# A recurrent attention with a token-mixing layer on one Trainium2 core: values of the last batch loaded like all others, ten output buffers, and a new order of 650 steps

## The chip, the core and the metric

The kernel runs on one core of one Trainium2 chip. A core has five engines with an instruction queue each: TensorE (PE in the profile; its weight loads are PEld) multiplies matrices and writes to the accumulator memory PSUM; VectorE (DVE), ScalarE (ACT) and GpSimd (POOL) compute on tiles in on-chip memory; SyncE (SP) here only issues transfers. Sixteen DMA engines carry the transfers between the chip's main memory and the on-chip memory. Every queue is worked in order: an instruction that waits holds all that stand behind it on its engine. The metric is the device time of one execution in microseconds (us), and the median of several runs counts.

## The reference

Four batches, eight heads, 768 tokens, 48 values to a head. The first layer is a recurrence with a decaying state, the second mixes tokens. Cut to what is computed:

```python
B, H, S, D = 4, 8, 768, 48
for t in range(S):
    cur = einsum('bhd,bhe->bhde', u * k[:, :, t], v[:, :, t])
    y[:, :, t] = einsum('bhd,bhde->bhe', r[:, :, t], state + cur)
    state = w[:, :, t, :, None] * state + einsum('bhd,bhe->bhde', k[:, :, t], v[:, :, t])
x = y.transpose(0, 2, 1, 3).reshape(B, S, H * D)
W_tok = einsum('bsd,btd->bst', x @ w_q, x @ w_k) / sqrt(64)
out = maximum(einsum('bst,btd->bsd', W_tok, x), 0) @ w_out
```

Inputs and output are float32; r, k, v and w have 4.7 MB each, and so has the output.

## The kernel before

**Units.** The work is cut into twelve units n = 0 to 11 of 256 tokens, three to a batch (n = 3b + i). A unit takes its tokens as two chunks c of 128. Its steps have names that stand here with their numbers: `kT_6` is the step kT of unit 6, `AM_6_1` the step AM of unit 6, chunk 1.

**First layer of a unit.** Four loads bring w, k, r and v (wg, kg, rg, vg, 384 KB each). ScalarE takes the logarithm (ln), TensorE sums it along the tokens (cw), ScalarE makes the two exponentials ep and en. Casts make k16, r16 and v16 in bf16; TensorE turns k and r (kT, rT). VectorE or ScalarE copies the turned k out of PSUM (ks), VectorE multiplies (qT, RT), and KT is ks (or the turned k in PSUM) times en, on GpSimd or VectorE. v must be permuted among partitions: TensorE does that (vp), and ScalarE copies the result out of PSUM (VB). dps and dd give the factors of the bonus, and Vd is VB times dd on GpSimd. Then A is the product of KT and RT for each chunk, AM masks it (VectorE), kb and kd turn KT back, sn and SB carry the state from chunk to chunk, yi and ya sum the output in PSUM, and X is that sum plus Vd. X is either an addition on VectorE, or TensorE adds Vd into PSUM (step yv) and ScalarE copies.

**Second layer.** xt and XT turn X, qk and QK project it (in the last unit the parts are wk, wq, wkc, wqc). When a batch has its three units, T and TS sum over the batch; then for each unit mx, a relu (rl), fp (the product with w_out), a copy os out of PSUM, and a store st. All the second half of a batch can be put off as long as buffers allow.

**Loads of v.** In units 0 to 8 v comes by `load`: two neighbouring tokens of a head are one run of 384 bytes, and vp permutes. The last batch is in `WHOLE` (line 170): there v comes by four transfers `load_whole` (lines 237 to 241), in runs of 192 bytes, already in permuted order, into one large tile vw of all three units; VB is then a cast from vw on GpSimd or ScalarE (lines 533 to 537) and there is neither v16 nor vp. k and r of all units but the first come by `load_long` in runs of 768 bytes.

**Buffers.** Loads have rings of four buffers (lines 194 to 201), so the load of unit n waits until unit n - 4 has read its buffer. The output tile os has a ring of four as well.

**Weights.** w_q and w_k (wts) and w_out (wo) are loaded on SP's queue, in two transfers each (rows 0 to 99 and 100 to 127) where the way is `T`, in one where it is `S` (lines 343 to 358). Both stand as `T`. wcast and ocast make them bf16.

**The order.** It is written out by hand in three tables (lines 84 to 134): `ORDER` lists the numbers of all steps in the order in which they are put on the engines' queues, `WAYS` the engine or form of each step that has a choice, and `BANKS` the PSUM bank of each tile there. A form `N` does nothing, `e` and `c` are other forms of the same step on TensorE, `d` is KT read from PSUM on VectorE. `WARM` (24) gives steps z, products with a tile of zeros, that keep TensorE busy; in this order 11 of them are done, the rest are `N`. Nine more stand ahead of all steps (line 873).

The queue of SP, decoded:

```
kg_0 wg_0 wg_1 rg_0 kg_1 kg_2 vg_0 rg_1 wg_2 vg_1 wg_3 rg_2 vg_2 kg_3 rg_3 wts vg_3 wg_4 wg_5
kg_4 rg_4 kg_5 rg_5 vg_4 wo wg_6 vg_5 wg_7 rg_6 kg_6 vg_6 kg_7 rg_7 vg_7 wg_8 kg_8 rg_8 wg_9 vg_8
kg_9 rg_9 kg_10 wg_10 rg_10 vw (4 transfers) st_0 wg_11 kg_11 rg_11 st_1 st_2 st_4 st_3 st_5 ...
```

At the end, VectorE does TS_11, four relus (rl_9_0, rl_9_1, rl_11_0, rl_11_1) and os_11_1; ScalarE does rl_10_0, rl_10_1, then os_9_0, os_10_0, os_10_1, os_9_1, os_11_0.

The lines that carry the choice of v, and the copy that follows:

```python
WHOLE = (B - 1,)
...
        if whole:
            VBs = add(("VB", n), "PA", lambda e: copy(
                e, view(VB.tile, 0, [[D, H], [DM, 2], [1, D]]),
                view(batch["vw"].tile, 2 * i * D, [[NCH * D, H], [D, 2], [1, D]])),
                batch["vwL"], VB, [batch["vw"]], cols=2 * DM)
```

Of the kernel before, what the change touches and what calls it, by code (L numbers as in the profile page):

```python
# [10 lines left out]
F32 = mybir.dt.float32  # L11
# [21 lines left out]
class Plan:  # L33
# [9 lines left out]
    def add(self, key, ways, fn, after=(), buf=None, reads=(), cols=0, mode=0, behind=None,  # L43
            half=-1, more=None):
        s = dict(key=key, ways=ways, way=ways[0], fn=fn, after=list(after), buf=buf,
                 reads=list(reads), cols=cols, mode=mode, behind=behind, half=half,
                 more=more or {}, i=len(self.steps), fills=False, out=False)
        if buf is not None:
            if buf.filler is None:
                buf.filler = s  # L50
                s["fills"] = True
                if buf.tile is None:
                    self.banks.append(buf)
                elif behind is None and buf.before is not None:
                    s["behind"] = buf.before.filler
            elif behind is None:
                s["behind"] = buf.filler
        self.steps.append(s)
        return s
# [22 lines left out]


ORDER = [
# [34 lines left out]
]  # L119
WAYS = (  # L120
    "PPDPPDPPDDDDDDPDTTPDDAAPPDPPPADDDEENDEAAPPDdPADEAEENDEAAAPAPPADEDcNDEDAAAAAAAAPADdPAAEAc"
    "cNDEADPPDdPAAeAcENDeDAPPDPPAAeAENDEAAAAAAAAAPPDPPAAEDEENDEAAPPDdPAAeAEENDEAAPPDPPAAEAcND"
    "EDAAADAAAAPPDPPAEAEcNDeAAPPDPPAeAccNDeDAPPDPPPAPPAENDEDADNDEAADDDDAAAAAADDADNNEEEENEEENE"
    "NENENNNNNNEN"
)
BANKS = [
# [7 lines left out]
]  # L134


WARM = 24

# [2 lines left out]
def kernel(  # L141
# [13 lines left out]
    B, H, S, D = r.shape  # L155
# [11 lines left out]
    N = B * NU  # L167

    LONG = tuple(range(1, N))
    WHOLE = (B - 1,)  # L170

    SHIFT = 25
    KAPPA = SHIFT * math.log(2.0)
# [11 lines left out]
    def const(shape, dtype, name):  # L185
# [6 lines left out]
    QW = NU * QS  # L192

    RINGS = dict(
        wg=(4, HW, F32), rg=(4, HW, F32), kg=(4, HW, F32), vg=(4, HW, F32), os=(4, 2 * DM, F32),
        kd=(2, KW, BF16), lw=(2, 1024, BF16), r16=(2, 1024, BF16), k16=(2, 1024, BF16),
        ep=(2, 8 * EW, BF16), en=(2, 1024, BF16), ks=(2, 1024, BF16), qT=(2, 1024, BF16),
        RT=(2, 1024, BF16), KT=(2, 1024, BF16), v16=(2, 2 * DM, BF16), VB=(2, 2 * DM, BF16),
# [139 lines left out]
    wts = {}  # L338

    def dma(key, fn, after=(), buf=None, reads=()):  # L340
        return add(key, "ST" if key[0] in ("wts", "wo") else "S", fn, after, buf, reads)

    def weights():
        def rows(e):
# [561 lines left out]
```

## Time and profile before

| what | value |
|---|---|
| median of 3 runs | 103.6 us |
| lowest, highest run | 101.3, 104.62 us |
| span of the profiled execution, first to last instruction | 101.1 us |
| moved by DMA in it | 24.68 MB, mean 244 GB/s |
| loads landed: median from issue, kg / wg / rg / vg | 5.5 / 6.3 / 6.4 / 6.9 us |
| stores landed: median from issue, 384 KB / 192 KB | 3.2 / 2.8 us |

The profile is of one execution. The page gives its span, and no time beside it; the runs differ from one another by 3.2%. In rows of groups, the first number behind the bar is the busy time of the group in us (overlaps taken out), the second the mean duration of one instruction in ns, and behind the second bar stands the time that the engine idled just before, with what ended it. In rows of time, the columns are start, duration, engine, line, operation, tiles, count, and in brackets the idle time before. In rows of stages, they are the stage, its length, the busy times of PE, PEld, DVE, ACT and POOL, the granted clock of TensorE, the share of the 16 DMA engines' time, and GB/s. The records of two instructions that follow one another on VectorE or ScalarE overlap by some 0.08 us, and a few matmul records are missing.

### The profile page before, as it was taken

What the parts mean: (1) busy time and instruction counts of PE and PEld (TensorE: products, weight loads), DVE (VectorE), ACT (ScalarE), POOL (GpSimd) and SP (SyncE); (2) the same over time, 40 slices, a digit from 0 to 9 for tenths busy, and PEclk for the clock granted to TensorE, in tenths of its full rate; (3) what the DMA queues carried; (4) which work ended last, traced back from release to release, by engine and by line L of the source; (5) the groups of instructions that cost most, each with busy time, mean ns of one, the idle gap of its engine ahead of it and who ended that gap; (6) DMA issues with size and microseconds to landing.
All of it is one profiled execution on the core that took longest, in us unless ns stands there. A gap on an engine that the chain in (4) does not pass through costs nothing.

```text
span 101.1 us, 4474 instructions
## 1 busy us (share of the span) xinstructions
PE 86.8 (86%) x1906; PEld 63.4 (63%) x1909; DVE 80.5 (80%) x134; ACT 80.9 (80%) x134; POOL 68.8 (68%) x82
## 2 busy tenths in 40 slices
PE   5966984989899888999899988999999998999920
PEld 1334553777597556678577875787877667776500
DVE  5423896899999989889999899999997897565520
ACT  5068975999799699599998999989997995735930
POOL 6858964699937764968899749999995897000000
PEclk9999999999999999999999999999999999999999
DMA  1999998999999999999999799999888831007591
GB/s 26 309 324 346 332 317 227 341 261 274 313 306 240 257 205 244 291 329 341 224 323 287 192 343 301 166 155 250 229 233 310 314 141 67 0 0 303 209 366 69
DMA packets 45165, 24.68 MB, mean 244 GB/s; under 512 B 31576, under 2 KB 43992, under 8 KB 45144
## 3 DMA queue, kind: packets, MB, share of 16 engines
q1 hardware_dynamic: 44984, 24.19, 86.9%
q8 instruction: 15, 0.25, 1.0%
q10 hardware_dynamic: 160, 0.20, 0.6%
q14 instruction: 6, 0.05, 0.2%
HBM read 19.66 MB, written 4.72 MB: 241 GB/s over the span
## 4 chain that ended last, share of the span: by engine, by line
PE 34%; ACT 15%; DMA 13%; DVE 12%; SPq 10%; issue 7%; POOL 4%; DVEq 0%; POOLq 0%; ACTq 0%
PE PS L177 34%; DMA vg<-in_v_dram 7%; DMA kg<-in_k_dram 6%; ACT ep L444 6%; SPq L227 5%; ACT en L451 4%; SPq L232 4%; DVE AM L592 3%; DVE X L724 2%; ACT os L275 2%; POOL v L281 2%; DVE ks L281 1%; POOL r L414 1%; DVE RT L513 1%; DVE qT L503 1%
## 5 line engine op out<-in xcount | busy, mean ns | idle before, releaser
L592 DVE TENSOR_TENSOR AM<-PS,US 128x1024 bf16<-128x1024 f32 x24 | 28.7, 1216 | 0.9 <-PE PS L177 0.6
L523 POOL TENSOR_TENSOR KT<-ks,en 128x1024 bf16<-128x1024 bf16 (+1 forms) x10 | 17.4, 1739 | 2.7 <-DVE qT L503 2.0
L572 POOL TENSOR_TENSOR Vd<-VB,dd 128x768 bf16<-128x768 bf16 (+1 forms) x14 | 18.0, 1292 | 1.5 <-ACT dd L275 1.0
L444 ACT ACTIVATE ep<-PS,kp 128x512 bf16<-128x512 f32 (+1 forms) x28 | 16.3, 646 | 0.1
L451 ACT ACTIVATE en<-PS,km 128x1024 bf16<-128x1024 f32 (+1 forms) x14 | 13.9, 1002 | 1.1 <-ACT QK L275 0.8
L724 DVE TENSOR_TENSOR X<-PS,Vd 128x768 bf16<-128x768 f32 (+1 forms) x13 | 11.6, 889 | 2.7 <-POOL Vd L572 1.4
L177 PE MATMUL PS<-wo,MX 128*128 128x384 bf16 x72 | 13.3, 326 | 0.2 <-ACT ep L444 0.2
L177 PEld LDWEIGHTS <-KT 48*128 48x128 bf16 (+1 forms) x312 | 10.3, 94 | 5.1 <-issue 2.6
L177 PE MATMUL PS<-RT,KT 48*128 48x128 bf16 x192 | 9.6, 217 | 1.9 <-POOL KT L523 1.0
L414 POOL CAST k<-kg 128x768 bf16<-128x768 f32 x10 | 8.2, 824 | 3.6 <-DMA kg<-in_k_dram 1.8
L281 DVE COPY ks<-PS 128x1024 bf16<-128x1024 bf16 x11 | 7.6, 689 | 3.7 <-PE PS L177 3.7
L275 ACT COPY os<-PS 128x768 f32<-128x768 f32 (+1 forms) x13 | 8.8, 679 | 1.9 <-PE PS L177 1.6
L414 POOL CAST r<-rg 128x768 bf16<-128x768 f32 x10 | 8.2, 824 | 3.1 <-DMA rg<-in_r_dram 1.9
L513 DVE TENSOR_TENSOR RT<-PS,ep 128x1024 bf16<-128x1024 bf16 (+1 forms) x14 | 8.5, 608 | 2.2 <-ACT ep L444 2.0
L403 ACT ACTIVATE lw<-wg 128x768 bf16<-128x768 f32 x12 | 10.1, 850 | 0.1
L177 PEld LDWEIGHTS <-MX 128*128 128x128 bf16 x72 | 6.4, 97 | 4.3 <-DVE MX L289 0.3
L287 ACT ACTIVATE MX<-PS 128x768 bf16<-128x768 f32 (+1 forms) x11 | 8.2, 758 | 0.9 <-PE PS L177 0.8
L275 ACT CAST VB<-PS 128x768 bf16<-128x768 f32 x9 | 7.3, 806 | 1.8 <-PE PS L177 1.7
L281 POOL CAST v<-vg 128x768 bf16<-128x768 f32 x9 | 7.4, 823 | 1.8 <-DMA vg<-in_v_dram 1.7
L177 PE MATMUL PS<-CM,lw 64*128 64x128 bf16 x192 | 7.9, 217 | 0.7 <-issue 0.4
L656 DVE TENSOR_TENSOR SB<-PS,ep 128x192 bf16<-128x192 f32 x20 | 7.0, 350 | 1.6 <-PE PS L177 1.5
L503 DVE TENSOR_TENSOR qT<-PS,ks 128x1024 bf16<-128x1024 bf16 x12 | 8.2, 681 | 0.0
(82 smaller groups left out, 182.8 us busy)
## 6 DMA issues: line engine op xcount, KB each, us to landing
kg<-in_k_dram SPq DMA_DIRECT2D x12, 384.0 KB, 5.5
wg<-in_w_dram SPq DMA_DIRECT2D x12, 384.0 KB, 6.3
rg<-in_r_dram SPq DMA_DIRECT2D x12, 384.0 KB, 6.4
vg<-in_v_dram SPq DMA_DIRECT2D x9, 384.0 KB, 6.9
out_dram<-os SPq DMA_DIRECT2D x9, 384.0 KB, 3.2
vw<-in_v_dram SPq DMA_DIRECT2D x4, 288.0 KB
out_dram<-os SPq DMA_DIRECT2D x5, 192.0 KB, 2.8
wof<-in_moe_w_out_dram SPq DMA_DIRECT2D x1, 450.0 KB
```

The lines of the kernel that those rows point to most:

```text
L177: return nc.tensor.matmul(o, l, rr, start=start, stop=stop, skip_group_check=True, is_transpose=trans)
L275: nc.scalar.copy(o, i)
L281: x.tensor_copy(o, i)
L403: nc.scalar.activation(view(lw.tile, 0, [[64, H], [512, 2], [1, D]]), view(g["wg"].tile, 0, [[D2, H], [D, 2], [1, D]]), ACT.Ln, bias=0.0, ...
L414: op(view(o.tile, 0, [[64, NP], [256, 4], [1, D]]), view(g[src].tile, 0, [[2 * D2, NP], [D, 4], [1, D]]))
L444: nc.scalar.activation(view(ep.tile, cs[0] * NP * EW + off, [[EW, NP * len(cs)], [step, 2], [1, 32]]), view(at(cw), cs[0] * 512 + j * 64, ...
L451: nc.scalar.activation(en.tile[:, ds(cs[0] * 512, w_)], at(cw)[:, ds(cs[0] * 512, w_)], ACT.Exp, bias=km, scale=-1.0)
L513: nc.vector.tensor_tensor(plain(RT.tile, cs, 32), turned(512, cs, True), plain(ep.tile, cs, EW // 4), ALU.mult)
L523: x.tensor_tensor(KT.tile[:, cols], ks.tile[:, cols], en.tile[:, cols], ALU.mult)
L572: (nc.vector if e == "D" else nc.gpsimd).tensor_tensor(Vd.tile[:, cols], VB.tile[:, cols], view(dd.tile, cs[0] * H, [[1, len(cs) * H], [0, ...
L592: AMs[c] = add(("AM", n, c), "D", lambda e, c=c, A=A: nc.vector.tensor_tensor(view(AM[c].tile, 0, [[C, 8], [1, C]]), view(at(A), 0, [[C, 8 ...
L724: nc.vector.tensor_tensor(o, y_, view(Vd.tile, c0 * DM, dims), ALU.add)
```

## The change

The last batch leaves `WHOLE`, so units 9 to 11 get loads vg, casts v16, products vp and copies VB like the others, and the four vw transfers and the tile vw are gone. The ring os has ten buffers. The weights are loaded by one transfer for each matrix. All three tables are new.

```diff
@@ ORDER, WAYS, BANKS @@
 ORDER = [
-    38, 15, 441, 301, 32, 18, 649, 644, 22, 539, 645, 2, 3, 26, 25, 0, 401, 581, 4, 5, 34, 33, 23,
...
+    37, 38, 39, 40, 86, 85, 87, 128, 88, 127, 129, 14, 21, 0, 2, 5, 12, 32, 22, 10, 4, 3, 7, 24,
...
@@ the kernel @@
     LONG = tuple(range(1, N))
-    WHOLE = (B - 1,)
+    WHOLE = ()
...
     RINGS = dict(
-        wg=(4, HW, F32), rg=(4, HW, F32), kg=(4, HW, F32), vg=(4, HW, F32), os=(4, 2 * DM, F32),
+        wg=(4, HW, F32), rg=(4, HW, F32), kg=(4, HW, F32), vg=(4, HW, F32), os=(10, 2 * DM, F32),
...
     def dma(key, fn, after=(), buf=None, reads=()):
-        return add(key, "ST" if key[0] in ("wts", "wo") else "S", fn, after, buf, reads)
+        return add(key, "S", fn, after, buf, reads)
```

The steps are numbered anew (657 instead of 652, since v now has five steps more). Decoded, SP's queue is:

```
wg_0 kg_0 rg_0 vg_0 kg_1 wg_1 rg_1 kg_2 vg_1 wg_2 rg_2 wg_3 vg_2 kg_3 rg_3 vg_3 wg_4 rg_4 kg_4 wts
wg_5 vg_4 rg_5 kg_5 vg_5 wg_6 kg_6 rg_6 wg_7 kg_7 vg_6 rg_7 vg_7 kg_8 wg_8 rg_8 vg_8 rg_9 wg_9 wg_10
rg_10 kg_9 kg_10 wo vg_9 wg_11 vg_10 vg_11 kg_11 rg_11 st_2 st_0 st_1 st_3 st_5 st_6 st_4 st_7 st_8 ...
```

What goes to which engine (number of steps before -> after, where it differs):

```
TensorE  vp 9 -> 12; yv done 0 -> 3; z done 11 -> 5; kb in form E 6 -> 3, e 7 -> 10;
         xt in form E 10 -> 8, e 3 -> 5; sn in form E 12 -> 11, c 8 -> 9
VectorE  KT 4 -> 7 (KT_0 in two halves among them); X 13 -> 10; dd 3 -> 7; kd 4 -> 6; wkc 0 -> 2;
         rl 4 halves -> 5 halves and 2 whole; os 1 whole and 1 half -> 3 halves; ks 11 -> 10;
         QK 1 -> 2; pads 2 -> 1; IU 1 -> 0
ScalarE  VB 9 -> 12; X 0 -> 3; rl 11 -> 8; kd 9 -> 7; dd 9 -> 5; os 13 -> 12; QK 10 -> 9; ks 1 -> 2;
         wkc 2 -> 0; k16 and r16 1 -> 0; v16 0 -> 1
GpSimd   KT 10 -> 7; VB 3 -> 0; v16 9 -> 11; k16 and r16 11 -> 12; pads 0 -> 1; IU 0 -> 1
```

IU makes the tile IDU, pads clears the tile kd. In the set-up, GpSimd now does 18 instructions ahead of k16_0 (ms_lw0, ms_ep1, ms_kp, ms_U, ms_I, as_C01, as_U1, as_C00, as_U2, ms_km, as_PM, as_ID, IU, pads_1, as_C10, as_C11, as_U0, as_U3; ms is a memset, as a selection by index).

TensorE's queue from the turn of k in unit 10 on, before and after (fp of units 9 and 11 comes in halves):

```
before  kT_10 rT_10 ya_8_1 ya_8_0 fp_3 mx_4 xt_7 xt_8 A_9_0 A_9_1 mx_5 qk_8 kb_9 A_10_0 dps_10 qk_7
        kb_10 sn_9_0 ya_9_0 ya_9_1 A_10_1 yi_9_1 fp_4 sn_9_1 cw_11 kT_11 sn_10_0 rT_11 yi_10_0
        ya_10_0 fp_5 ya_10_1 yi_10_1 xt_9 sn_10_1 T_8 A_11_0 kb_11 xt_10 dps_11 qk_9 mx_6 sn_11_0
        A_11_1 yi_11_0 ya_11_0 mx_7 qk_10 mx_8 yi_11_1 ya_11_1 fp_6 xt_11_0 xt_11_1 fp_7 wk_11_1
        wq_11_1 wk_11_0 wq_11_0 T_11_0 T_11_5 T_11_4 fp_8 mx_9 mx_10 mx_11 fp_9_0 fp_10_0 fp_10_1
        fp_9_1 fp_11_0 fp_11_1
after   kT_10 rT_10 xt_8 fp_1 A_9_1 vp_9 mx_3 fp_2 sn_9_0 A_10_0 dps_10 vp_10 mx_5 sn_9_1 A_9_0 cw_11
        kb_10 fp_0 A_10_1 sn_10_0 qk_8 ya_9_0 ya_9_1 kT_11 yi_9_1 rT_11 fp_5 yi_10_0 yi_10_1 ya_10_0
        ya_10_1 vp_11 T_8 sn_10_1 xt_9 A_11_1 kb_11 fp_3 sn_11_0 dps_11 A_11_0 xt_10 yi_11_0 yi_11_1
        qk_9 ya_11_1 mx_6 qk_10 ya_11_0 mx_4 fp_6 xt_11_0 xt_11_1 mx_7 fp_4 wk_11_0 wk_11_1 mx_8 fp_7
        T_11_0 T_11_4 T_11_5 wq_11_0 wq_11_1 fp_8 mx_11 mx_10 mx_9 fp_11_0 fp_10_0 fp_10_1 fp_11_1
        fp_9_0 fp_9_1
```

On GpSimd, ocast stands behind k16_10 and ahead of v16_9, KT_10 and v16_10. At the end VectorE does TS_11, wqc_11_0, wqc_11_1, rl_11_0, rl_10_0, rl_10_1, os_10_0, rl_9_0, rl_9_1, os_9_0, os_9_1, and ScalarE rl_11_1, os_11_0, os_10_1, os_11_1.

More of the change, by code (lines that the diff above doesn't have):

```diff
@@ L84 @@
 ORDER = [
[34 rows of a table removed]
[36 rows of a table added]
 ]
 WAYS = (
[L121 to L124, printed above, removed]
+    "PPDDPDPDDDDPDPPPPDPAAPPDddPAADDcEEAeAAPPAdPAAeDEEEAEDAPPDdPADeAcEAEAAAAAAAAAPPDdPAAEAEEN"
+    "DeDDPPDdPADeDccNDEAAPPDPAADeAcNDEDAADAAAAAPPDPPAAEAEcNDEAAPPDPPADeAEENDEAAPPDPPADeDcNDeA"
+    "AAAADAAAPPDdPADEAEENDeDDPPDPPAAeDccNDeAAPPAPPPADPPAENDEDDDNDEADDDDDDDDDDADAAANNNENNNNNEN"
+    "NNNNENNENNENN"
 )
 BANKS = [
[7 rows of a table removed]
[7 rows of a table added]
 ]
```

82 rows, old and new, of tables (BANKS, ORDER) are left out of this document.

## The prediction

> **What bounds the kernel now.** I read the page first (busy shares, slices, the chain), then busy time by stage, then the engines in order of time where a stage leaves room. From the page:
>
> ```profile
> span 101.1 us, 4474 instructions
> PE 86.8 (86%) x1906; PEld 63.4 (63%) x1909; DVE 80.5 (80%) x134; ACT 80.9 (80%) x134; POOL 68.8 (68%) x82
> ...
> PE 34%; ACT 15%; DMA 13%; DVE 12%; SPq 10%; issue 7%; POOL 4%; DVEq 0%; POOLq 0%; ACTq 0%
> ```
>
> No engine bounds it alone. The chain changes hands all the time, and its DMA and SP-queue parts (13% and 10%) say that loads matter somewhere. Where, the stages tell (us, then each engine's busy time, the granted clock, the DMA share):
>
> ```profile
> 0.00:6.00 6.00, 4.45 (x10) 1.35 (x10) 2.52 (x13) 1.32 (x2) 4.72 (x20) 1.00 0.73 192
> 6.00:20.00 14.00, 10.37 (x253) 7.63 (x258) 9.73 (x19) 12.01 (x20) 9.62 (x14) 1.00 1.08 313
> 20.00:40.00 20.00, 17.86 (x473) 13.68 (x469) 19.47 (x31) 18.53 (x30) 14.77 (x15) 1.00 1.07 262
> 40.00:60.00 20.00, 18.74 (x471) 14.70 (x470) 18.19 (x27) 18.15 (x30) 16.38 (x16) 1.00 1.01 292
> 60.00:78.00 18.00, 17.38 (x421) 13.48 (x419) 17.21 (x23) 16.76 (x29) 16.51 (x15) 1.00 1.02 237
> 78.00:88.00 10.00, 9.27 (x233) 7.27 (x228) 8.06 (x14) 8.24 (x17) 6.82 (x7) 1.00 0.37 140
> 88.00:101.10 13.10, 8.72 (x75) 5.32 (x70) 5.33 (x11) 5.95 (x13) 0.00 (x0) 1.00 0.49 183
> ```
>
> From 20 to 88 us TensorE is busy 63.25 of 68 us, VectorE is nearly as full, and until 78 the DMA engines are full too. There, little is to be won, and every added microsecond on TensorE or VectorE costs nearly one. The room lies in the first 20 us: from 6 to 20 TensorE idles 3.63 us. The stalls there:
>
> ```profile
> 1.24 4.45 PE L177 MATMUL PS<-Z 128*128 128x512 bf16 x10 [1.24 <-DVE Z L872]
> 6.62 0.41 PE L177 MATMUL PS<-PM,k 64*128 64x64 bf16 x16 [0.94 <-POOL PM L301]
> ...
> 10.02 0.40 PE L177 MATMUL PS<-RT,KT 48*128 48x128 bf16 x8 [0.71 <-POOL KT L523]
> ...
> 11.24 0.59 PE L177 MATMUL PS<-Z 128*128 128x512 bf16 x2
> ...
> 17.36 0.36 PE L177 MATMUL PS<-v,PM 64*64 64x384 bf16 x4 [1.36 <-POOL v L281]
> ```
>
> ```profile
> 8.02 0.82 POOL L417 CAST r<-rg 128x768 bf16<-128x768 f32 x1 [1.45 <-DMA rg<-in_r_dram]
> 8.81 1.15 POOL L523 TENSOR_TENSOR KT<-ks,en 128x512 bf16<-128x512 bf16 x1
> ...
> 13.15 0.83 POOL L414 CAST r<-rg 128x768 bf16<-128x768 f32 x1 [0.39 <-DMA rg<-in_r_dram]
> ...
> 16.49 0.82 POOL L281 CAST v<-vg 128x768 bf16<-128x768 f32 x1 [1.29 <-DMA vg<-in_v_dram]
> 17.27 0.83 POOL L572 TENSOR_TENSOR Vd<-VB,dd 128x384 bf16<-128x384 bf16 x1
> ```
>
> ```profile
> 18.13 0.96 DVE L724 TENSOR_TENSOR X<-PS,Vd 128x768 bf16<-128x768 f32 x1 [0.99 <-POOL Vd L572]
> ```
>
> These casts began when their loads landed: rg_0 (the fourth issued) at 8.02, rg_1 (the eighth) at 13.15, so 1.28 us a load. The cast of vg_1 (the tenth) at 16.49 holds the queue of GpSimd: behind it stands Vd_0_1, for which X_0 waits.
>
> **Part (a), the start, -3.0 us.** The new order issues wg_0, kg_0, rg_0, vg_0 first, rg_1 seventh, vg_1 ninth. KT_0 moves from GpSimd (1.15 us a half) to VectorE (0.42, the row of equal shape below), so the 0.71 us wait at 10.02 goes. vg_1 lands about one load, 1.3 us, earlier, which takes the 1.36 us wait of TensorE. Vd_0_0 and Vd_0_1 now stand ahead of v16_1 on GpSimd, so the 0.99 us wait of X_0 goes, and X_0 itself moves to ScalarE. Together 3.06; I take -3.0. What is late next: k16_0 stands behind 18 set-up instructions of GpSimd (pads_1 and IDU are moved there, the memset of CM away). In the old order it began at 5.24 (row below); I expect about 1.1 us later. ln_0 gains about as much, since wg_0 is issued first and not second, so RT_0 is nearly where it was. Ends: -5 (most of the 3.63 idle and of the warm-up matmuls' time in this stage goes) and +1.1 (only the late k16_0 counts).
>
> ```profile
> 5.24 0.82 POOL L417 CAST k<-kg 128x768 bf16<-128x768 f32 x1
> ...
> 39.18 1.15 POOL L281 CAST wo<-wof 128x1152 bf16<-128x1152 f32 x1 [1.78 <-DMA wof<-in_moe_w_out_dram]
> ...
> 76.42 0.83 POOL L414 CAST k<-kg 128x768 bf16<-128x768 f32 x1 [0.51 <-DMA kg<-in_k_dram]
> 77.90 0.83 POOL L414 CAST r<-rg 128x768 bf16<-128x768 f32 x1 [0.66 <-DMA rg<-in_r_dram]
> ```
>
> ```profile
> 60.00:64.00 4.00, 3.45 (x71) 2.40 (x69) 4.00 (x6) 3.89 (x8) 4.00 (x5) 1.00 1.16 265
> 64.00:68.00 4.00, 4.00 (x123) 3.24 (x124) 3.82 (x7) 3.68 (x8) 4.00 (x4) 1.00 1.09 165
> ```
>
> **Part (b), the loads, -1.0 us.** The four vw loads carry 1.18 MB in runs of 192 bytes; where they move (64 to 68) the full DMA engines give 165 GB/s, against 313 from 6 to 20. As three vg loads they would take 1.18 MB / 313 = 3.8 instead of 7.2 us, 3.4 us of DMA time less. The store st_0, which stood ahead of wg_11 on SP's queue, moves behind all loads, 0.39 MB or 1.3 us. So rg_11 could land near 73 instead of 77.9. That is mostly hidden: GpSimd waited only 0.51 and 0.66 us for these last loads. I take -0.5 for the end, and -0.5 for wo, which goes from the middle of the loads to their last eight, so that GpSimd no longer stands 1.78 us for it at 37 to 39 (KT_5 was queued behind). Ends 0 and -2.5. Issuing the weights whole takes three issues off SP's queue (SP runs ahead): nothing. Ten output buffers: no engine's row shows a copy waiting for a store, so nothing here; they only allow the stores to be late. What stands behind: all 4.72 MB of output now go out behind rg_11, 15 us of DMA time at 313 GB/s, in the last 25 us, where DMA shares were 0.37 and 0.49; so hidden, but for the last store as before.
>
> **Part (c), the moved wait for wo, +0.4 us.** ocast now stands on GpSimd ahead of v16_9, KT_10 and v16_10, and on TensorE's queue fp_1, the first product with wo, stands ahead of A_9_1 and all of batch 3. Some 41 loads lie between the fourth and wo; at 1.43 us each (44 loads, the weights and the rest from 8.02 to 77.90) wo lands near 66 us, and kT_10 would come near 64. Ends 0 and +2.5; the wait of 1.78 above is the nearest row, and as TensorE's own work in the stage moves with it I take a quarter.
>
> **Part (d), added work, +1.6 us.** Rows by shape (busy is that of the group, overlaps taken out):
>
> ```profile
> L177 PE MATMUL PS<-v,PM 64*64 64x384 bf16 x36 | 3.2, 345 | 1.7 <-POOL v L281 1.4 <-ACT ep L444 0.3
> L177 PE MATMUL PS<-ID,X 128*128 128x128 bf16 x54 | 4.3, 219 | 0.5 <-ACT dd L275 0.3 <-DVE X L724 0.2
> L177 PE MATMUL PS<-QK,TS 128*128 128x256 bf16 x36 | 5.6, 273 | 0.4 <-ACT TS L275 0.3
> L177 PE MATMUL PS<-ID,KT 128*128 128x128 bf16 x40 | 3.2, 218 | 0.1
> L177 PE MATMUL PS<-ID,KT 48*128 48x48 bf16 x80 | 2.3, 181 | 0.1
> L177 PE MATMUL PS<-wo,MX 128*128 128x384 bf16 x72 | 13.3, 326 | 0.2 <-ACT ep L444 0.2
> ...
> L513 DVE TENSOR_TENSOR RT<-PS,ep 128x512 bf16<-128x512 bf16 x4 | 1.7, 419 | 2.0 <-ACT ep L444 2.0
> L518 DVE TENSOR_TENSOR KT<-PS,en 128x1024 bf16<-128x1024 bf16 x4 | 2.7, 680 | 0.0
> L724 DVE TENSOR_TENSOR X<-PS,Vd 128x768 bf16<-128x768 f32 x11 | 10.5, 950 | 1.6 <-POOL Vd L572 1.4
> ...
> L275 ACT CAST VB<-PS 128x768 bf16<-128x768 f32 x9 | 7.3, 806 | 1.8 <-PE PS L177 1.7
> ```
>
> TensorE: three vp steps of 4 matmuls, 12 x 3.2/36 = +1.07; three yv steps of 4 matmuls with 192 columns, between 0.080 (128 columns) and 0.156 (256), by columns 0.118 each, +1.4; kb three times in the short form, 3 x (8 x 0.080 - 16 x 0.029) = -0.5; xt likewise about -0.3. Together +1.65. Six warm-up matmuls fewer count nothing: they stood where TensorE waits. VectorE: KT five whole and two halves instead of four whole, +1.5; X -2.85; four more dd and two wkc, small copies, +1.1; relus two whole (0.95, as X) and one half (0.55, the last os copy of part (e)) more, +2.45; kd four whole (0.55, between the two bf16 rows) and two halves (0.35) instead of one and three, +1.3; one ks, one pads, IDU less, one QK and half an os more, -0.9; less 0.08 of overlap on ten more instructions: +1.8. ScalarE: VB +2.4 and X +2.4 against fewer relus, kd and os: about 0. GpSimd loses three KT. The two additions run side by side, and I count them once, +1.6; ends 0 (in idle time) and +3.4 (one behind the other).
>
> **Part (e), the tail, -0.3 us.**
>
> ```profile
> 91.58 0.56 DVE L281 CAST TS<-PS 128x384 bf16<-128x384 f32 x1
> ...
> 96.88 0.56 DVE L281 COPY os<-PS 128x384 f32<-128x384 f32 x1 [1.86 <-ACT os L275]
> ```
>
> ```profile
> 94.39 2.47 ACT L275 COPY os<-PS 128x384 f32<-128x384 f32 x5
> ```
>
> Five half copies in a row on ScalarE, then one on VectorE; now it is three and three, about -0.9. But wqc_11_0 and wqc_11_1 now stand behind TS_11 on VectorE, ahead of mx_11: two small copies, 0.3 each by estimate (a half copy takes 0.56), +0.6. Ends -1 and +2 (outputs put off, below).
>
> **The sum.** -3.0 - 1.0 + 0.4 + 1.6 - 0.3 = -2.3 on the execution shown, whose span is 101.1 us; what lies around the span the page doesn't say (the lowest of the three runs is 101.3). The median of the runs, 103.6, lies 2.5 above that span. I put the change on the median: 103.6 - 2.3 = 101.3 us. A measurement of this kernel tells about 2% (2.1 us) from no change, so this is faster by a hair.
>
> **The rivals.** (1) Additions in series: TensorE and VectorE are both near full from 20 on and hand work to each other, so +1.65 and +1.8 add up. 103.6 - 2.3 + 1.8 = 103.1, no change. For it: 19.47 of 20 us busy on VectorE; against it: the 1.6 to 3.6 us idle of TensorE before 40.
> (2) Outputs put off, slower: behind kT_11 on TensorE stand two fp, one mx and one vp more than before, 2 x 6 x 13.3/72 + 3 x 5.6/36 + 0.36 = 3.05 us. If kT_11 comes no earlier than it did (k16_11 ended at 77.25), that is the loss: 103.6 + 3.05 - 0.3 = 106.35. It decides if kT_11 comes after about 76.5. For it: DMA shares of 1.0 to 78 us; against it: 4.7 us less DMA time ahead of rg_11.
> (3) wo late in full: +2.5 for +0.4, 103.4, no change.
> (4) A cold array: three or four warm-up matmuls, not eleven, stand between the steps of the first 20 us. The first ten took 4.45 us, 0.445 each, a later pair 0.59, 0.295 each. Were unit 0 and 1 run at the first pace, some 7.9 us of other work from 6 to 20 (10.37 less seven warm-up matmuls at 0.36) would take up to 1.5 times as long; if two thirds of these 3.9 us show and the rest falls into waits, that is 103.9, no change. The granted clock reads 1.00 in all stages, which speaks against it. [...]
>
> **Chances.** Forecast 0.50 (0.46 beyond 2%, 0.04 within); rival 1 0.23, rival 3 0.08, rival 4 0.05, all within 2%; rival 2 0.14 (0.13 beyond 2%, 0.01 within). Faster 0.46, same 0.41, slower 0.13. Range: from the ends of (a) and (b) at about half their way, 98.0, to 104.8, which takes in rivals 1, 3 and 4 and leaves out rival 2 and the best ends.
>
> **What would show it.** (a) second AM of unit 1 ending near 19 us (21.7 before), no wait of X_0 for Vd. (b) kg_11's cast near 73 and no wait before it; DMA above 230 GB/s to the end of the loads. (c) GpSimd's wait for wof and TensorE's before fp_1. (d) TensorE's busy time within 1 us of 86.8. (e) the last os copy 5 us or less after TS_11. I am wrong if TensorE's idle from 6 to 40 stays near 5.8 us, or if kT_11 isn't earlier than 76.5.

## The result: 111.9 us where 101.3 were forecast

| | median | lowest to highest | runs |
|---|---|---|---|
| before | 102.85 us | 101.3 to 104.62 | 4 |
| after | 111.94 us | 111.53 to 113.74 | 4 |

The ratio is 1.098 (95% interval 1.088 to 1.108): slower, and outside the range 98.0 to 104.8. The execution in the profile is the longest of the four, 113.74 us with a span of 112.0, so its stages carry 1.8 us that the median doesn't have. Ratios, here and below, compare only executions within 1.5% of the fastest of their kernel; medians are of all.

### The profile page after: what moved, and what is told of

Read it like the earlier page. It is cut to its first block, busy times and chain, and to the rows that moved or that the text cites. A ratio compares the mean times of both kernels' runs of the same rounds, so it can differ in the third digit from the quotient of the medians.

```text
span 112.0 us, 4567 instructions
## 1 busy us (share of the span) xinstructions
PE 95.8 (85%) x1956; PEld 70.9 (63%) x1956; DVE 82.5 (74%) x143; ACT 81.9 (73%) x127; POOL 66.3 (59%) x83
## 4 chain that ended last, share of the span: by engine, by line
PE 54%; DVE 27%; POOL 7%; issue 5%; ACT 3%; DVEq 0%; POOLq 0%
PE PS L178 54%; DVE AM L593 6%; DVE ks L282 4%; DVE qT L504 3%; DVE KT L519 3%; DVE X L725 2%; DVE RT L514 2%; POOL KT L524 2%; DVE MX L290 2%; DVE os L282 1%; POOL US L302 1%; POOL CM L302 1%; ACT os L276 1%; DVE SB L657 1%; POOL kd L247 1%
## 5 line engine op out<-in xcount | busy, mean ns | idle before, releaser
L524 POOL TENSOR_TENSOR KT<-ks,en 128x1024 bf16<-128x1024 bf16 (+1 forms) x7 | 12.9, 1851 | 6.8 <-DVE ks L282 5.0
L178 PEld LDWEIGHTS <-KT 48*128 48x128 bf16 (+1 forms) x328 | 11.3, 105 | 6.0 <-issue 3.4
L276 ACT CAST VB<-PS 128x768 bf16<-128x768 f32 x12 | 9.6, 800 | 3.1 <-PE PS L178 2.7
L178 PE MATMUL PS<-RT,KT 48*128 48x128 bf16 x192 | 10.9, 246 | 0.9 <-DVE X L725 0.4
L725 DVE TENSOR_TENSOR X<-PS,Vd 128x768 bf16<-128x768 f32 (+1 forms) x10 | 8.6, 872 | 2.6 <-PE PS L178 2.6
L178 PE MATMUL PS<-CM,lw 64*128 64x128 bf16 x192 | 9.6, 248 | 0.8 <-POOL CM L302 0.6
L519 DVE TENSOR_TENSOR KT<-PS,en 128x1024 bf16<-128x1024 bf16 (+1 forms) x7 | 4.2, 607 | 7.8 <-PE PS L178 7.8
L282 POOL CAST v<-vg 128x768 bf16<-128x768 f32 x11 | 9.1, 826 | 0.0
L178 PEld LDWEIGHTS <-lw 64*128 64x128 bf16 x192 | 7.3, 109 | 2.8 <-issue 2.3
L178 PE MATMUL PS<-VB,AM 128*128 128x48 bf16 x192 | 8.4, 191 | 0.7 <-issue 0.6
```

The lines of the kernel that those rows point to most:

```text
L178: return nc.tensor.matmul(o, l, rr, start=start, stop=stop, skip_group_check=True, is_transpose=trans)
L276: nc.scalar.copy(o, i)
L282: x.tensor_copy(o, i)
L524: x.tensor_tensor(KT.tile[:, cols], ks.tile[:, cols], en.tile[:, cols], ALU.mult)
L725: nc.vector.tensor_tensor(o, y_, view(Vd.tile, c0 * DM, dims), ALU.add)
```

## The profile after

From the page of the kernel after: span, busy times, the clock granted to TensorE in 40 slices, and the chain.

```profile
span 112.0 us, 4567 instructions
PE 95.8 (85%) x1956; PEld 70.9 (63%) x1956; DVE 82.5 (74%) x143; ACT 81.9 (73%) x127; POOL 66.3 (59%) x83
PEclk9996555555555589999999999999999999999999
PE 54%; DVE 27%; POOL 7%; issue 5%; ACT 3%; DVEq 0%; POOLq 0%
```

Two things differ from the page of before. The DMA and SP parts of the chain (13% and 10%) are gone: nothing on it waits for a load. And VectorE's part has gone from 12% to 27%: TensorE and VectorE now hand the work to and fro. The stages of the kernel after (columns as before the change):

```profile
6.00:20.00 14.00, 10.77 (x218) 7.72 (x219) 8.15 (x17) 8.53 (x17) 9.11 (x15) 0.61 1.07 309
20.00:40.00 20.00, 18.52 (x343) 14.62 (x338) 14.23 (x20) 13.39 (x20) 9.72 (x11) 0.50 1.04 293
40.00:60.00 20.00, 17.59 (x494) 14.37 (x492) 18.25 (x29) 18.18 (x29) 15.25 (x15) 1.00 1.00 291
60.00:78.00 18.00, 15.48 (x425) 12.58 (x423) 16.21 (x27) 17.08 (x27) 15.44 (x14) 1.00 0.52 151
78.00:88.00 10.00, 9.84 (x228) 7.30 (x220) 8.98 (x14) 9.00 (x16) 8.12 (x7) 1.00 0.14 54
```

From 20 to 40 us VectorE does 20 instructions where it did 31, and TensorE, at a granted clock of 0.50 where it was 1.00, 343 matmul records where it did 473. From 60 to 78 the DMA share is 0.52: the loads have landed by about 70 us, 8 us sooner than before, and AM_8 still ends 4 us later (table below). TensorE's waits, from its timeline in the kernel after (start, duration, operation, tiles, count, idle time ahead):

```profile
8.00 0.41 PE L178 MATMUL PS<-PM,k 64*128 64x64 bf16 x16 [1.09 <-POOL k L418]
...
9.92 0.34 PE L178 MATMUL PS<-ID,KT 48*128 48x48 bf16 x8 [0.59 <-DVE KT L519]
...
11.53 0.34 PE L178 MATMUL PS<-ID,KT 48*128 48x48 bf16 x8 [1.26 <-DVE kd L284]
...
24.70 0.61 PE L178 MATMUL PS<-PM,r 64*128 64x64 bf16 x16 [0.47 <-DVE KT L519]
...
33.59 0.61 PE L178 MATMUL PS<-PM,r 64*128 64x64 bf16 x16 [0.97 <-DVE KT L519]
...
42.27 0.27 PE L178 MATMUL PS<-SB,RT 48*128 48x48 bf16 x8 [1.05 <-DVE SB L657]
...
76.70 0.27 PE L178 MATMUL PS<-SB,RT 48*128 48x48 bf16 x8 [1.32 <-DVE SB L657]
```

The first three rows are unit 0: kT_0 waits for the cast of k (below, from GpSimd's timeline), and both halves of kb_0, which stand ahead of A_0_0, wait for VectorE. The rows at 24.70 and 33.59 are rT_2 and rT_3: they wait for KT, which doesn't feed them. Before, only four waits of 0.4 us or more stood between 6 and 100 us (3.4 us in all); now there are nine (7.9).

```profile
7.12 0.82 POOL L418 CAST k<-kg 128x768 bf16<-128x768 f32 x1
```

Where the units stand, from the traces of these kernels and of some below (end of the second masking AM of a unit, end of X_11, span, in us; one profiled execution each):

| kernel | AM_1 | AM_3 | AM_5 | AM_7 | AM_8 | AM_10 | X_11 | span |
|---|---|---|---|---|---|---|---|---|
| before | 21.7 | 35.5 | 49.2 | 63.5 | 69.1 | 77.5 | 88.8 | 101.1 |
| after | 22.8 | 39.2 | 55.7 | 66.5 | 73.2 | 87.4 | 98.0 | 112.0 |
| a1 (more warm-up) | 21.6 | 34.0 | 53.0 | 64.7 | 71.4 | 87.2 | 97.8 | 111.9 |
| d1 (rT behind kT) | 22.9 | 34.0 | 49.5 | 60.4 | 68.0 | 81.0 | 91.4 | 105.5 |
| s1 (d1, start mended) | 21.1 | 32.7 | 48.5 | 59.4 | 68.2 | 81.5 | 92.0 | 106.0 |
| e4 (after, outputs cut) | 23.6 | 36.4 | 53.6 | 64.5 | 70.6 | 84.8 | 95.7 | 109.7 |
| f1 (before, weights whole, ten buffers) | 21.6 | 35.4 | 47.9 | 62.2 | 67.9 | 76.2 | 86.8 | 99.2 |
| c3 (values in the old order) | 21.6 | 35.9 | 48.8 | 63.0 | 68.7 | 79.6 | 92.1 | 104.9 |

Single executions scatter: e4 is the same program as the kernel after up to AM_8, and yet it stands 2.8 us ahead of it at AM_3.

## The experiments

Each gives the median of its runs; "before" is the kernel before on the same chip. The changed kernel itself was run only in the first measurement, so a difference from its 111.94 mostly compares two chips; over the chips the median of the kernel before went from 102.44 to 105.44.

### Is it the clock?

**a1_after_z:** the changed kernel with 20 warm-up products between the steps instead of 5.

```diff
-cw_0 kT_0 z z rT_0 kb_0_0 kb_0_1 vp_0 A_0_0 uT z sn_0_0 kT_1 ...
+cw_0 z z z kT_0 z z rT_0 z z z kb_0_0 z z z z z kb_0_1 z vp_0 A_0_0 uT z z sn_0_0 kT_1 z ...
```

> The changed kernel with 20 warm-up products instead of 5, 19 of them in TensorE's waits of the first 20 us; nothing else is changed. Clock theory (the sparse start lets the array fall to half clock from 10 to 41 us, which costs the changed kernel about 6.5 us by the end of unit 5): the granted clock stays at 1.00 and the time falls by 5 to 7 us, to 105 to 107 us. Order theory (the clock is a side effect and the order of the later units holds the time): the clock may rise but the time stays within 2 us of 111.9.

111.94 us (111.38 to 113.58), ratio 1.094 (1.081 to 1.108). The page of a1:

```profile
PEclk9999999999999955899999999996799999999997
```

The granted clock is 1.00 from 6 to 20 us and 0.97 from 20 to 40 (0.61 and 0.50 in the kernel after), unit 3 is 5.2 us earlier than in the kernel after, and by unit 10 all of it is gone. **b1_before_noz** is the reverse, the kernel before with none of its 11 products between the steps:

> The kernel before with none of its 11 warm-up products between steps. Clock theory: the array falls to half clock in the first 40 us here too, and the time rises by 4 to 8 us, to 107 to 111. Order theory: the products stand in waits only, the time stays at 103 within 2 us.

102.73 us over 10 runs, ratio 1.000 (0.994 to 1.006). In both orders the warm-up products buy nothing. The single executions say the same of the clock itself: in b1 six ran at a mean clock of 0.907 to 0.932 and took 101.68 to 104.0 us, four at 0.968 to 1.000 took 102.03 to 107.53; of the changed kernel's own, one at 0.883 took 111.53 us and one at 0.981 took 111.68.

### One part alone: loads, buffers, values

**f1_before_whole:** the old order and values, with the weights whole and ten output buffers.

```diff
-os=(4, 2 * DM, F32)
+os=(10, 2 * DM, F32)
-return add(key, "ST" if key[0] in ("wts", "wo") else "S", fn, after, buf, reads)
+return add(key, "S", fn, after, buf, reads)
```

> The kernel before with two parts of the change alone: weights in single transfers and ten output buffers; order, banks and the values of the last batch as before. Theory (these two parts are worth a little, since the small transfers are cheaper and nothing in the order waits on more): 101 to 102.5 us, the wait of the GpSimd queue for the second half of the loads shorter. Rival (the loads' time was hidden, as the trace after suggests, where the loads landed 8 us earlier and bought nothing): 102.8 us, within 0.5 of the kernel before. Rival (the smaller transfers had been better): 103.5 or more.

101.74 us over 12 runs against 102.69 over 17; ratio 1.000 (0.994 to 1.005). Between the first theory and the rival "hidden" it can't be decided, and that small transfers are cheaper is not shown; a loss of more than about half a us is excluded.

**a2_after_os4:** the changed kernel with the old four output buffers.

> The changed kernel with four output buffers instead of ten; the order is the same. If the buffers do nothing, as predicted, 111.9 us within 1%, and the run is at the same time a second draw of the clock. If the late stores need them, copies to os wait for stores and it is 1 to 4 us slower.

118.71 us, ratio 1.161 (1.143 to 1.179). Stores stand so late in this order that the copies wait for them, 15.3 us in two groups of the waits of a2 (engine, tile, what it waited for: total, times, longest):

```profile
ACT os L268 <- DMA out_dram<-os: 9.0, 2, 8.5
...
DVE os L274 <- DMA out_dram<-os: 6.3, 1, 6.3
```

So ten buffers are a need of the new order, no gain by themselves. With four, five copies (os_4 to os_8) stand in the order ahead of the store that would empty their buffer, so this kernel doesn't store all of the output that the reference has; its time prices the waits alone.

**c2_old_order:** the changed source (values loaded and permuted like the others, ten buffers, weights whole) in the order of before, the new steps put in by hand. An earlier attempt, c1_before_v, loaded the values of unit 11 into a buffer that unit 7 had yet to read; its 126.1 us tell nothing of the change.

```diff
-... VB_9 (GpSimd, from vw) Vd_9 VB_10 k16_11 r16_11 Vd_10 KT_11_0 KT_11_1 VB_11 Vd_11
+... v16_9 KT_10 Vd_9 v16_10 k16_11 r16_11 Vd_10 KT_11_0 v16_11 KT_11_1 Vd_11
+TensorE: vp_9 ahead of A_9_0, vp_10 behind mx_5, vp_11 behind mx_6; VB on ScalarE
```

> All of the change but the order: the values of the last batch as two-token runs with cast, vp and copy, ten output buffers, weights in single transfers, in the order of the kernel before (the new steps put by hand where the old copies stood). If the new order is what costs: 102 to 105 us, within 2% of before. If the values' path costs (1.07 us of TensorE, 2.4 us of ScalarE and a longer chain from load to copy in the last batch): 107 us or more.

107.52 us (106.94 to 108.04). Its units run 1.3 us ahead of before up to unit 8 and lose everything in units 9 to 11. Two further placements followed.

> As c2_old_order (the changed source in the order of before), with the casts of the values of units 10 and 11 freed from the queue that held them: GpSimd's cast of unit 10 stands ahead of KT_10 instead of behind Vd_9, ScalarE makes the cast of unit 11 behind ep_11. c2 took 107.5 us, 4.7 above before, and lost all of it in units 9 to 11. Theory (the new path of the values costs only its work, 1.1 us of TensorE; the rest was my placing): 103.5 to 105. Rival (the longer way of the values, a cast, a product and a copy where one copy was, costs 4 to 5 us in the last units whatever the placing): 106.5 to 108.

> As c3 (the changed source in the order of before; 106.8 us), with the products and copies of the values set earlier: vp_10 and VB_10 ahead of mx_5, v16_11 on GpSimd ahead of Vd_10, vp_11 behind the first half of unit 10's output and VB_11 behind it, 17 steps of TensorE earlier than in c3. In c3 TensorE waited 0.90 us before vp_10 for the bank and 0.71 us before the state product of unit 11 for VB_11, which ended at 88.0 us, 6 us later than in f1. Theory (placement, the work alone is 1.1 us): 103.3 to 104.5 us. Rival (the added cast, product and copy hold GpSimd, ScalarE and a pair of banks in a stage that has none to spare): 106 to 107.5.

c3: 106.76 us, ratio 1.047 (1.037 to 1.058). c4: 108.01 us (105.92 to 108.88). Moving the wait moved the loss. TensorE's timeline, c3 first, then c4:

```profile
73.07 0.49 PE L170 MATMUL PS<-QK,TS 128*128 128x256 bf16 x3 [0.48 <-ACT VB L268]
...
74.46 0.36 PE L170 MATMUL PS<-v,PM 64*64 64x384 bf16 x4 [0.90 <-ACT MX L280]
...
88.02 0.36 PE L170 MATMUL PS<-VB,kd 128*128 128x48 bf16 x8 [0.71 <-ACT VB L268]
```

```profile
72.87 0.36 PE L170 MATMUL PS<-v,PM 64*64 64x384 bf16 x4 [0.71 <-ACT VB L268]
...
74.19 0.49 PE L170 MATMUL PS<-QK,TS 128*128 128x256 bf16 x3 [0.63 <-ACT VB L268]
...
84.39 0.35 PE L170 MATMUL PS<-v,PM 64*64 64x384 bf16 x3 [0.97 <-ACT ep L437]
```

Five of the six waits, 0.48 to 0.97 us, are for PSUM: vp and its neighbours need a pair of banks, and in units 9 to 11 of the old order the pair is still being read by ScalarE. The row at 88.02 is another kind: there sn_11 waits for VB_11 itself. In the old order, then, the new path of the values costs 4 to 6 us, not its 1.07 us of TensorE's time. From AM_8 to X_11 c3 takes 23.4 us where f1 takes 18.9; TensorE is 1.6 us more busy there and idles 2.9 more. That PSUM is the reason of all of it is argued from these rows, not tested.

**e2_d1_whole** takes the values' part back in the new order (base d1, below):

> As d1_kr (the changed kernel with rT behind kT), with the values of the last batch loaded in the unit's own row order and not permuted, as before: three casts on GpSimd and twelve products less, ScalarE's copies of VB_9 to VB_11 read the loaded tile. d1 took 107.6 us. Theory (TensorE is full from 64 us on in d1, so what it is spared there is time): 1.07 us of vp less, 106.2 to 106.9 us. Rival (the values' path is what holds the last units): 103 to 105. Rival (it lay beside other work): 107.6, within 0.5.

109.37 us (108.22 to 111.53), no faster than its base at 107.62 and 109.23 (below). As these two differ by 1.6 us, the theory's 1 us can't be excluded, but 103 to 105 can: in the new order, where the path has its place, it isn't what holds the last units.

### The order: rT held by the readers of kT

**d1_kr:** the changed kernel with rT directly behind kT on TensorE in units 1 to 6, 8, 9 and 11. For unit 3:

```diff
-kT_3 sn_2_0 z xt_1 yi_2_0 rT_3
+kT_3 rT_3 sn_2_0 z xt_1 yi_2_0
```

> The changed kernel with rT right behind kT on TensorE's queue in units 1 to 6, 8, 9 and 11, as most units of the kernel before have it; the other queues are unchanged. Theory that rT is held by VectorE's reads of kT in the same bank (rT_2 and rT_3 waited 0.5 to 1.6 us for KT in the traces): the waits go and the time falls by 2 to 4 us, to 108 to 110. Theory that the waits only move (TensorE and VectorE wait for one another for want of other work): within 1% of 111.9.

107.62 us (106.85 to 109.44), 4.3 less than the changed kernel. Three misses went with it or after it. **d2_out_early** set wo and the outputs of batch 0 early again: 116.85 us, 4.9 more. The loads aren't the reason: no engine waits for one behind the start, and the last is issued at 63.6 us, after 64.9 in the changed kernel. It falls behind from AM_5 to AM_7, where the products put early now stand (14.3 us, 10.9 in the changed kernel). And from AM_8 to AM_10, from where they are gone, it takes 14.8 us, no less than the changed kernel's 14.2: the outputs of batch 0 are not what makes that stretch long.

> The changed kernel with w_out loaded behind vg_5, its cast behind KT_5, and the output products and copies of batch 0 (fp and os of units 0, 2 and 1) put right behind their relus instead of between units 9 and 10. Theory that the put-off outputs are missing as filler while engines wait for one another from 20 to 65 us, and are paid in full later: the time falls by 3 us or more (three products of 1.11 us on TensorE), to 109 or less. If those waits can't be filled: within 1% of 111.9.

**d3_ktP** gave KT_1 to KT_4 to GpSimd: 113.06 us, 1.1 more. Each takes 2.1 us there, 0.7 on VectorE, and TensorE waited 2.9 us in five places for KT from GpSimd.

> The changed kernel with KT of units 1 to 4 on GpSimd (2.13 us each) instead of VectorE (0.68 us each, read from PSUM). Theory that the serial chain of VectorE (ks, KT, RT, qT, then A on TensorE) sets the pace of the first units: GpSimd has the time there (about half idle from 20 to 40 us), 1 to 3 us faster. If KT's latency counts: 2 to 5 us slower.

**e3_d1_short_fp** cut work from d1 and took 110.92 us, 3.3 more, though it was 2.5 us behind d1 at unit 3, long before its first difference.

> As d1_kr, with the output product of the three units of batch 0 (fp_0, fp_1, fp_2) cut from six matmuls to two, so that their rows of the output hold a third of the sum only. In d1 these three stand among units 9 to 11 at 72.0, 74.2 and 78.2 us, 1.15 us each; before they stood ahead of 58 us. Cut, they give TensorE back 3 x 0.76 = 2.3 us. Theory (put-off outputs are in series with the last units, TensorE bound from 64 us on): 105.0 to 105.6 us, 2.0 to 2.6 less than d1. Rival (VectorE's chain of AM, KT, ks, qT, RT sets the pace of units 9 and 10 and TensorE only looks full): 107 to 107.6.

So d1 was run again beside two halves of its edit.

> The same kernel as d1_kr once more, beside its neighbours on one chip. e3 with 2.3 us less work took 3 us longer than d1, and was 2.5 us behind it at unit 3, 36 us before its first difference. Theory (d1's 107.6 is sound and e3's loss belongs to e3): 107 to 108.3 us. Rival (times of this order scatter by some 3 us with the chip or the layout of the program): 109 to 111.

> The changed kernel with rT moved directly behind kT on TensorE in units 2 and 3 alone, the two units whose rT shows a wait for VectorE's reading of kT in the trace after (0.47 and 0.97 us). Theory (the wait itself, and what VectorE then loses by it, is d1's gain of 4.3 us): 108 to 109 us. Rival (the gain of d1 lies in the later units, where rT simply comes earlier): 111.5 or more.

> The same move in units 4, 5, 6, 8, 9 and 11 alone. Theory (the hold in units 2 and 3): 111 to 112 us, as the changed kernel. Rival (rT earlier in the later units): 108 to 109. Rival (neither, d1's gain was one of layout): both h1 and h2 at 110 to 112, with no sum of 4.

d1 again: 109.23 us (108.15 to 111.5), ratio 1.070 (1.042 to 1.097). h1: 110.97 (108.31 to 113.15). h2: 109.50 (108.24 to 110.71), ratio 1.068 (1.046 to 1.090). Two measurements of one kernel differ by 1.6 us, so d1's gain is some 3.5 us (111.94 less the mean of 107.62 and 109.23), with h1 1.0 and h2 2.4 of it; h1's runs lie 4.8 us apart, so its share isn't firm. The expectation that the hold in units 2 and 3 was nearly all is a miss. Each half removes its own waits, as the timelines show, h1 first (it keeps those for SB), then h2 (it keeps those of rT_2 and rT_3):

```profile
37.51 0.27 PE L170 MATMUL PS<-SB,RT 48*128 48x48 bf16 x8 [1.05 <-DVE SB L649]
...
73.42 0.28 PE L170 MATMUL PS<-SB,RT 48*128 48x48 bf16 x8 [1.31 <-DVE SB L649]
```

```profile
25.49 0.41 PE L170 MATMUL PS<-PM,r 64*128 64x64 bf16 x16 [0.60 <-DVE KT L511]
...
32.06 0.41 PE L170 MATMUL PS<-PM,r 64*128 64x64 bf16 x16 [1.36 <-DVE KT L511]
```

In units 4 and 9 the hold runs the other way. There kT, rT and then the reader of kT stand in this order, and the reader waits for rT, which it doesn't read. In the kernel after kT_4 ended at 39.82 and kT_9 at 72.81, but ks_4 and KT_9 began only behind rT:

```profile
40.81 0.41 PE L178 MATMUL PS<-PM,r 64*128 64x64 bf16 x16
41.26 0.69 DVE L282 COPY ks<-PS 128x1024 bf16<-128x1024 bf16 x1 [2.10 <-PE PS L178]
...
73.85 0.41 PE L178 MATMUL PS<-PM,r 64*128 64x64 bf16 x16
74.37 0.69 DVE L519 TENSOR_TENSOR KT<-PS,en 128x1024 bf16<-128x1024 bf16 x1 [1.17 <-PE PS L178]
```

SB stands behind them on VectorE, hence TensorE's two waits for SB (1.05 and 1.32 us), which h1 keeps too. In d1 and h2, where rT stands directly behind kT, the two readers begin without these waits.

### The start

**s1_start:** d1, with k16_0 and A_0_0 freed.

```diff
-GpSimd:  ... as_ID IU pads_1 as_C10 as_C11 as_U0 as_U3 k16_0
+GpSimd:  ... as_ID as_C10 as_C11 as_U0 as_U3 k16_0      (IU, pads_1 on VectorE, behind ms_k160)
-TensorE: rT_0 kb_0_0 kb_0_1 vp_0 A_0_0 uT z sn_0_0 kT_1 dps_0 A_0_1
+TensorE: rT_0 kb_0_0 vp_0 A_0_0 uT z sn_0_0 kT_1 dps_0 A_0_1 kb_0_1
```

> d1 (the changed kernel with rT behind kT; 107.6 and 109.2 us in two calls) with the start mended: pads_1 and IDU from GpSimd to VectorE, so that k16_0 starts near 5.3 us and not at 7.1, and the second half of kb_0 behind A_0_1, so that A_0_0 doesn't stand behind the wait for kd_0_0 (1.26 us). Theory (the late start is carried to the end, since TensorE and VectorE follow each other unit by unit): AM_1 ends near 20.5 us instead of 22.9, and 105.5 to 107 us. Rival (it is taken up by slack in the units behind): AM_1 earlier by as much, and 108 to 109.5 us.

106.44 us (104.95 to 107.73), ratio 1.038 (1.029 to 1.048): 2.0 us less than the mean of d1's two medians, little more than the 1.6 by which these differ. AM_1 ends at 21.1. GpSimd's timeline in s1 shows the cast where it was in the old order, now waiting for its load:

```profile
5.54 0.82 POOL L410 CAST k<-kg 128x768 bf16<-128x768 f32 x1 [0.29 <-DMA kg<-in_k_dram]
```

### What is left: units 9 and 10

Up to unit 7, s1 runs 4.1 us ahead of the kernel before; from AM_7 to AM_8 it takes 8.8 us where before took 5.7 (1.6 of it a stall, last section), and from AM_8 to AM_10 13.3 where before took 8.4, and the kernel after 14.2. In every profile of the new order this second stretch takes 13.0 to 15.8 us; in the three of the old order with the values as before (before, b1, f1) 8.4. From AM_10 on they are nearly alike (before 23.6 us to the end, after 24.6, s1 24.5). Were it TensorE alone, cutting its work there should show:

> The changed kernel with fp_0, fp_1 and fp_2 cut from six matmuls to two, as e3 does to d1 (their rows of the output hold a third of the sum). Theory (the put-off outputs stand in series with the last units): 109.4 to 110 us, 2 to 2.5 less than the changed kernel. Rival (they fill time that TensorE has anyway): 111.5 to 112.5. If it is slower, as e3 was, then work taken away costs time in this order, and the series theory falls for good.

111.34 us (111.05 to 111.44), 0.6 less of the 2 expected, which is within the difference of two measurements of one kernel; the stretch takes 14.2 us still. The stretch in stage rows: before, after, e4.

```profile
69.10:77.50 8.40, 8.33 (x166) 6.34 (x164) 8.14 (x11) 7.58 (x13) 7.31 (x6) 1.00 0.93 261
```

```profile
73.20:87.40 14.20, 12.67 (x289) 9.79 (x289) 12.34 (x19) 13.07 (x23) 10.57 (x11) 1.00 0.08 31
```

```profile
70.60:84.80 14.20, 12.16 (x267) 9.04 (x267) 12.27 (x20) 12.66 (x22) 10.91 (x11) 0.88 0.08 30
```

In the same two units TensorE has 4.3 us more to do than before, VectorE 4.2 and ScalarE 5.5. Work has been put off into this stretch on all three, so cutting it on one leaves the others. VectorE stays 12.3 to 12.5 us busy in it in after, e4, d2, s1 and d1; whether it sets the pace isn't tested. Nor do the engines overlap as well: the chain of d1 there reads, in order of time (start, duration, engine and tile):

```profile
67.94 0.69 DVE KT L511
68.63 0.61 DVE ks L274
69.24 0.02 issue
69.27 0.69 DVE qT L496
69.96 0.27 DVE SB L649
70.23 0.04 issue
70.27 1.60 PE PS L170 x56
71.87 0.02 issue
71.89 0.69 DVE ks L274
72.59 0.59 DVE RT L506
73.18 0.39 DVE qT L496
```

KT_9, ks_9 and qT_9 stand behind AM_8 on VectorE, and kT_9 behind A_8_1 on TensorE; in the old order ks_9, qT_9 and RT_9 stood ahead of AM_8_0. The last 4 us (106.4 less 102.4) arise from AM_7 to AM_10, where s1 loses some 8 us, having been 4.1 ahead; which part is the later preparation of unit 9 and which the work put off stays open. Drawing kT_9 forward wasn't tried: no pair of PSUM banks is free there, as A_8_0, A_8_1, xt_7 and cw_9 stand in all four that BANKS gives out (banks 0 to 7).

## Why the prediction was wrong, by its steps

- **Part (a), the start, -3.0: the step that failed first.** AM_1 was to end near 19 us; it ended at 22.8, after 21.7 before. The late k16_0 was sized at 1.1 us and is 1.9 (7.12 against 5.24). The two halves of kb_0 ahead of A_0_0 were not looked at: 1.85 us of waits. s1 mends both and gains 2.0 us. The three waits that part (a) listed (0.71, 1.36 and 0.99) did go; new ones stand ahead of them. IDU and pads_1 alone take 1.7 us of GpSimd (3.93 to 5.66). TensorE's own queue of unit 0 wasn't gone through.
- **What no part priced: the order of units 1 to 10.** "There, little is to be won" was taken from full engines, and then nothing to be lost either was assumed. rT set apart from kT costs some 3.5 us (d1, twice). The rest, about 4 us, arises from AM_7 to AM_10, and its cause is open. (3.5, 2.0 and 4.0 add up to 9.5 where 9.1 were measured; they are differences of medians from several chips.)
- **Part (b), loads, -1.0.** The mechanism was right (landed by 70 us instead of 77.9), its worth was not: in the kernel after no engine waits for a load behind the start, and the end comes 9 us later. f1 doesn't test it, since its values load as before; it shows weights loaded whole to be worth half a us at most. c2 loads the values as the kernel after does, in the old order, and stands at AM_8 where f1 does (67.8 and 67.9).
- **Part (c), wo, +0.4.** No wait for wof appears in the kernel after: ocast began at 73.97, just behind the cast ahead of it. Zero, and rival 3 with it.
- **Part (d), +1.6.** The work was there, and somewhat more of it. VectorE's came as forecast, 82.5 us busy after 80.5. TensorE's groups in d1, which ran at a mean clock of 0.945 (columns as before the change):

```profile
L170 PE MATMUL PS<-v,PM 64*64 64x384 bf16 x48 | 4.5, 362 | 0.0
...
L170 PE MATMUL PS<-ID,X 128*128 128x128 bf16 x42 | 3.5, 219 | 0.3 <-DVE SB L649 0.2 <-issue 0.2
L170 PE MATMUL PS<-ID,KT 48*128 48x48 bf16 x112 | 3.5, 185 | 2.5 <-DVE kd L276 1.3 <-DVE KT L511 0.8 <-POOL KT L516 0.3
...
L170 PE MATMUL PS<-ID,KT 128*128 128x128 bf16 x24 | 1.8, 220 | 0.3 <-ACT X L715 0.3
L170 PE MATMUL PS<-ID,X 64*128 64x64 bf16 x60 | 1.7, 191 | 0.1
L170 PE MATMUL PS<-Vd,ID 128*128 128x192 bf16 x12 | 1.6, 259 | 0.0
```

  vp is +1.3 (3.2 before), yv +1.6, kb and xt together -0.3 (10.5 after 10.8): +2.6 where 1.65 was forecast, a part of it, by estimate, from the granted clock, 0.63 from 6 to 20 us in d1 and 1.00 before. As a price in the end it can't be read: taking vp back in e2 gave nothing beyond the scatter.
- **Part (e), tail, -0.3.** From X_11 to the end 14.0 us against 12.3: +1.7, near its upper end. The last copy of os ended 6.5 us behind the start of TS_11 (102.05 to 108.56), not 5; before it was 5.9.
- **Rival 1, additions in series, 103.1.** Both additions came, +2.6 on TensorE and +2.0 on VectorE, but they can't carry 9 us.
- **Rival 2, outputs put off, 106.35.** It came nearest and its condition was met: kT_11 began at 87.4, far behind 76.5, which the prediction had named as a sign of being wrong. But its price was TensorE's alone, in the tail. What the order put off lies earlier and on three engines, and in e4 TensorE's share was worth 0.6 us, within the scatter. Its number came nearest, but not by its reason.
- **Rival 4, a cold array, 103.9.** Half of it came: the granted clock reads 0.50 from 9 to 40 us. The end didn't follow, as a1 shows. Over the 90 executions of the changed kernel and of those made for the experiments, each compared with its own kernel, a mean clock lower by 0.05 went with 0.4% of time (correlation -0.22).

## What to carry to other kernels

Go through every engine's queue of a new order unit by unit, and price a step that moves apart from its partner as you would an added wait: here rT moved apart from kT cost some 3.5 us, more than the 1.6 forecast for all added work. In this kernel two tiles in one pair of PSUM banks that weren't written back to back held each other both ways: the second write waited for the readers of the first (rT, 0.47 to 1.58 us), or the reader of the first for the second write (ks_4 2.10, KT_9 1.17 us). Loads that landed earlier, by 70 us instead of 77.9, were worth only the waits that they spared: no engine was left waiting for one behind the start, and the end came 9 us later. Work cut from one engine, where the other two were as full, gave 0.6 of 2 us (e4).

## What the runs showed of the hardware

**In this program a bank is one thing to wait for.** rT writes other columns than kT, and still waited 0.47 (kernel after) to 1.58 us (a1) for VectorE's reading of kT in the same banks; the other way, ks_4 and KT_9 waited 2.10 and 1.17 us for rT. These are semaphore waits that the program carries: the runs show what it costs to guard by bank, not what the chip would do without.

**The clock stayed low under load.** In the kernel after the granted clock was 0.50 from 20 to 40 us while TensorE was busy 18.52 of 20 us, its longest wait 0.97; rT's 16 products took 0.61 us there and 0.41 where the clock was 1.00. The clock read 0.50 from about 9 us on and 1.00 again from 40 on; no run shows what held it low for so long.

**A stall without a cause in the profile.** In eight executions of seven kernels of the new order TensorE stopped inside one run of 16 weight loads, for 0.56 to 2.55 us, at the same place in the program (ya_7). TensorE's and its weight loader's timeline in d1:

```profile
61.74 0.10 PEld L170 LDWEIGHTS <-AM 128*128 128x128 bf16 x1
...
63.35 0.56 PE L170 MATMUL PS<-VB,AM 128*128 128x48 bf16 x16 [1.54 <-issue]
63.35 0.45 PEld L170 LDWEIGHTS <-AM 128*128 128x128 bf16 x15 [1.51 <-issue]
```

No semaphore is waited for that the profile shows. Something lies near in time: packets of 16 KB on the DMA queue that the profile names "instruction". In d1 one of them ended at 61.94, and TensorE went on at 63.35, 1.41 us later. All 24 such stalls of 0.4 us or more that stand behind 14 us, in the 20 traces, end 1.27 to 1.61 us after the end of such a packet; an execution has 15 of them. That TensorE waited for its next instructions is likely from this, and no run tests it.
